# A weight piece loaded as two half transfers, and one head's keys apart from its queries, in an attention kernel

## The chip, the cores and the metric

The kernel runs on one core of one Trainium2 chip. The metric is the device time of one execution in microseconds (us); less is better. The engines are PE (TensorE, matrix multiply), DVE (VectorE), ACT (ScalarE), POOL (GpSimd) and SP (SyncE, which here issues nearly all DMA transfers).

## The reference

Attention over 8 batches, 8 heads, 576 positions and 64 channels, with a bias that is computed from the distance of two positions, and behind it a gated feed-forward layer over all 4608 tokens, whose weights come as 64-bit floats.

```python
scores = scale * np.matmul(q, k.transpose(0, 1, 3, 2)) + bias
attn = np.exp(scores - np.max(scores, axis=-1, keepdims=True))
attn = attn / (np.sum(attn, axis=-1, keepdims=True) + 1e-09)
x = np.matmul(attn, v)          # then heads side by side: (4608, 512)
a = x @ w1
b = x @ w2
h = a * b @ w3
out = (h @ w_out).astype(np.float32)
```

## The kernel before

The kernel has three parts. First the bias of all heads is computed and stored to DRAM (`nb_d`), then comes the attention, and then the feed-forward layer, which keeps PE busy to the end. The change touches the attention only.

**Units.** The attention runs through 32 units: a unit is a pair of heads and one batch. Scores of a unit come in nine tiles, named 0 to 7 and M: an even number belongs to the first head, an odd one to the second, and M holds the last 64 rows of both. For each tile there is a step S (PE: scores from q and k, `op_S`, L332), T (DVE: adds the bias and finds the extreme of each row, L343) and E (ACT: the exponential and its sum, L368). Two tiles at a time are transposed by DVE (R, L378). PE multiplies the transposed tiles with v in the next unit (W0 to W4, L428), ACT copies the product x out of PSUM (X, L437 and L442), and SP stores it (xd, L448).

**Loads.** A unit needs q0 and k0 (first head), q1 and k1 (second head), and v in five parts v0 to v4 (128 or 96 KB), which SP loads with one transfer each (L315), one to two units ahead. POOL copies the lower 64 partitions of a v part to the upper ones (L320). Buffers of q and k stand twice, so a load waits until the scores two units earlier have read them. Most units also load a row of the next pair's bias (L296).

**Weight pieces.** 24 of the 32 units prepare one piece of the weights w_out and w3 (128 x 512 numbers of 64 bits, 512 KB) in nine steps, c0 to c8, made by `narrow`. c0 (`fetch`, L182) is the transfer into `wi`. c1 to c3 run on ACT: the Abs of the high words (`size`, L187), the Copy of the low words (L191), the Sign (L194). c4 to c8 run on POOL (a clamp, three doublings, a sum and a product). Units whose number leaves 0 or 7 when divided by 8 have no piece.

**Order.** The order of all steps is written out by hand. `rhythm` gives each step of a unit a time and an engine, in us from the unit's start (T0), with a unit length of 12.17 us (PERIOD); `arrange` puts the units one behind the other, and every engine, SP's queue too, gets its steps sorted by these times. The times only set the order: an engine that reaches a step waits for what it needs, and all behind it on that engine waits with it. On SP, before: k1 at 9.80, q1 at 9.90 (two units ahead), v2 at 9.85, v3 at 12.10, c0 at 0.2 of the next unit, which is 12.37, v4 at 1.98 of it, xd at 2.80, v0 at 4.55, k0 at 5.50 and q0 at 5.60.

Of the kernel before, what the change touches and what calls it, by code (L numbers as in the profile page):

```python
# [10 lines left out]
I32 = mybir.dt.int32  # L11
# [6 lines left out]
P = 128  # L18
# [13 lines left out]
PERIOD = 12.17  # L32
# [43 lines left out]
def rhythm(tiles, turns):  # L76

    at = {}
    for n, t in enumerate(tiles):
        at["S" + t] = S_AT[n], "PE"  # L80
        at["T" + t] = T_AT[n], "DVE"
        at["E" + t] = E_AT[n], "ACT"
    for n, ts in enumerate(turns):
        at["R" + ts] = R_AT[n], "DVE"
    for n, t in zip("abc", (2.70, 3.36, 4.00)):
        at["r" + n] = PERIOD + t, "DVE"
    at["rd"] = PERIOD + 5.30, "SP"
    for n, w in enumerate(W_AT):
        at[f"W{n}"] = PERIOD + w, "PE"
        at[f"lv{n}"] = w + 1.90 - PERIOD, "SP"  # L90
        at[f"V{n}"] = V_AT[n], "POOL"
    at["X"] = 2 * PERIOD + 0.70, "ACT"
    at["xd"] = 2 * PERIOD + 2.80, "SP"
    for h in range(2):
        for k, n in enumerate("kq"):
            at[f"l{n}{h}"] = -2 * PERIOD + (5.50, 9.80)[h] + 0.1 * k, "SP"
    at["c0"] = 0.2, "SP"
    at["c1"] = 5.60, "ACT"
    at["c2"] = 8.15, "ACT"
    at["c3"] = 11.65, "ACT"  # L100
    at["c4"] = 6.30, "POOL"
    for n, t in zip("567", AT_TWICE):
        at["c" + n] = t, "POOL"
    at["c8"] = 12.80, "POOL"
    return at


def arrange(NU, pieces):

    at = [rhythm(TILES, ("02", "46", "M", "13", "57")) for u in range(NU)]  # L110
    begin(at)
    for n, w in enumerate(W_LAST):
        at[-1][f"W{n}"] = w, "PE"
    at[-1]["X"] = X_LAST, "ACT"
    at[-1]["xd"] = X_LAST + 1.00, "SP"
    for u in range(NU - PER_PAIR):
        b = u % PER_PAIR
        at[u]["n" + TILES[b]] = AT_N, "SP"
        if b == PER_PAIR - 1:
            at[u]["n" + TILES[-1]] = PERIOD + AT_N_LAST, "SP"  # L120
    for k, n in enumerate(("lk0", "lq0")):
        at[2][n] = -2 * PERIOD + 9.60 + 0.1 * k, "SP"
    return {
        (n, u): (u * PERIOD + t + 1.4, e) for u in range(NU) for n, (t, e) in at[u].items() if n[0] != "c" or u in pieces
    }
# [3 lines left out]
def relpos_attention_moe(  # L129
# [17 lines left out]
    nc = tc.nc  # L147
# [3 lines left out]
    NTOK, DO = out.shape  # L151
# [4 lines left out]
    SQ = 8.0  # L156
    assert SQ * SQ == D

    def f(ap):
        return ap.bitcast(F32)  # L160

# [3 lines left out]
    WIDE = moe_w1.dtype == mybir.dt.int64  # L165
    LEAST = struct.unpack("<f", struct.pack("<I", 0x38000000))[0]
    MOST = struct.unpack("<f", struct.pack("<I", 0x47EFFFFF))[0]

    def narrow(pool, src, n, x, queue, pieces=1, clamps=nc.vector, signed=False):

        d = {}

        def cut(ap):
            return ap if pieces == 1 else ap.rearrange("p (c n) -> p c n", c=pieces)

        def fetch():
            if not WIDE:
                queue.dma_start(cut(x), src)
                return
            wi = pool.tile([P, n, 2], I32, name="wi")  # L180
            flat = wi.rearrange("p n t -> p (n t)")
            queue.dma_start(cut(flat), src.bitcast(I32))  # L182
            mag = pool.tile([P, n], F32, name="wmag")
            d.update(lo=wi[:, :, 0], hi=wi[:, :, 1], mag=mag, bits=mag.bitcast(I32))

        def size():
            nc.scalar.activation(d["mag"], f(d["hi"]), AF.Abs)  # L187

        def rest():

            nc.scalar.activation(x, d["lo"].bitcast(U32), AF.Copy, scale=2.0 ** -51, bias=2.0)  # L191

        def sign():
            nc.scalar.activation(f(d["hi"]), f(d["hi"]), AF.Sign)  # L194

        def clamp():
            clamps.tensor_scalar(d["mag"], d["mag"], LEAST, MOST, op0=ALU.max, op1=ALU.min)

        def shift():

            nc.vector.tensor_scalar(d["bits"], d["bits"], 3, None, op0=ALU.logical_shift_left)

        def total():

            nc.gpsimd.tensor_tensor(x.bitcast(I32), x.bitcast(I32), d["bits"], op=ALU.add)
            if not signed:
                nc.gpsimd.tensor_tensor(x, x, f(d["hi"]), op=ALU.mult)

        def mark():

            nc.vector.scalar_tensor_tensor(
                x.bitcast(I32), d["hi"], -2 ** 31, x.bitcast(I32), op0=ALU.bitwise_and, op1=ALU.bitwise_xor,
            )

        def twice():

            nc.gpsimd.tensor_tensor(d["bits"], d["bits"], d["bits"], op=ALU.add)  # L217

        steps = [fetch, size, rest, sign, clamp, shift, total]
        if signed:  # L220
            steps = [fetch, size, rest, clamp, shift, mark, total]
        if clamps is nc.gpsimd:
            steps = steps[:5] + [twice] * 3 + [total]
        return steps if WIDE else [fetch] + [lambda: None] * (len(steps) - 1)

    def drive(plan, *more):
# [15 lines left out]
    w3s = [[held.tile([P, DO], F32, name=f"w3s{t}_{hf}") for hf in range(2)] for t in range(NF)]  # L242
    wos = [held.tile([P, DO], F32, name=f"wos{t}") for t in range(NF)]
    cva = ctx.enter_context(tc.tile_pool(name="cva", bufs=2))
# [14 lines left out]
    vp = []  # L259
    units = [(p, b) for p in range(NPAIR) for b in range(B)]  # L260
    NU = len(units)
    lo, hi = slice(0, 64), slice(64, 128)
    NB = {}
    st = {u: {} for u in range(NU)}

# [84 lines left out]
    for i in range(2):  # L350
        t = att.enter_context(tc.tile_pool(name=f"sums{i}", bufs=1)).tile([P, 64], F32, name=f"sums{i}")
# [98 lines left out]

    def piece_of(i):
        if i < NF:
            return narrow(cva, moe_w_out[i * P:(i + 1) * P, :], DO, wos[i], nc.sync, clamps=nc.gpsimd)
        hf, t = divmod(i - NF, NF)
        return narrow(cva, moe_w3[t * P:(t + 1) * P, hf * DO:(hf + 1) * DO], DO, w3s[t][hf], nc.sync, clamps=nc.gpsimd)

    pieces = dict(zip([u for u in range(NU) if 0 < u % B < B - 1], (piece_of(i) for i in range(3 * NF))))
    assert len(pieces) == 3 * NF

# [20 lines left out]
    with ExitStack() as pro:  # L480
# [29 lines left out]
        def reach(G):  # L510

            return (G + 1) * GR - 1, S - 1 - G * GR
# [9 lines left out]
        for G in range(NGRP):  # L522
            n = max(reach(G)) + 1
# [42 lines left out]
        for G in range(NGRP):  # L566
            at = -LEAD + G * PACE_B
# [38 lines left out]
    def fetch_w(t, m):  # L606

        if m == 0:
            big[t] = bg.tile([P, 4, 2 * P], F32, name="big")
        flat = big[t].rearrange("p s n -> p (s n)")  # L610
        src = (moe_w1, moe_w2)[m].rearrange("(c p) n -> p c n", p=P)[:, :, t * P:(t + 1) * P]
        for step in narrow(cva, src, NC * P, flat[:, m * NC * P:(m + 1) * NC * P], nc.sync, pieces=NC, signed=True):
            step()
            yield
# [242 lines left out]
    for i in range(2 * NF):  # L857
        hf, t = divmod(i, NF)
# [16 lines left out]
    for t in range(NF):  # L875
        t0 = t_f + STEP0 * (t - 3) - LEAD_W * max(0, 3 - t)
        for m, (at0, d) in enumerate((((2.70, 3.35, 3.40, 3.80, 4.10, 4.90), -7.0), ((7.00, 7.65, 7.70, 8.00, 8.40, 9.40), -0.8))):
            size, rest, clamp, shift, mark, total = at0
# [11 lines left out]
    for n in range(NPR * NF):  # L890
# [3 lines left out]
        if p == 0:  # L894
            for j, u in AT_U.items():
                for m in range(2):
                    at(t0 + u + 2.08 * m, plain, cs, j, m)
                for k, d in AT_G.items():
                    if n == 0 and k + j == "gc":
                        d = AT_GC  # L900
# [18 lines left out]
        elif 0 < p < NPR - 1 and ft in (2, 5):  # L919
            i = int(ft > 4)  # L920
# [87 lines left out]
```

## Time and profile before

| | before |
|---|---|
| median of three runs | 1077.39 us (1069.25 to 1078.34) |
| the profiled execution | 1073.51 us |
| its span, first to last instruction | 1071.6 us |
| PE busy (share of the span) | 1038.9 us (97%) |
| DVE | 780.5 us (73%) |
| ACT | 557.4 us (52%) |
| POOL | 318.1 us (30%) |
| moved by DMA | 218.36 MB, mean 204 GB/s |

The shares are averages over the whole span. DVE is busy nine tenths or more of the time through the attention and far less in the feed-forward part, so the attention is to be read by itself. A wait in the views below is idle time of an engine, with what ended it; "issue" stands where nothing that the profile shows ended it. The engines read their instructions by DMA too: q8 is the queue of such transfers, 110 packets of together 1.80 MB in this execution, beside the data queue q1.

### The profile page before, as it was taken

The page shows a single profiled execution, that of the slowest core. Times are in us where ns is not written, and L with a number is a line of the kernel's source. Part 1 is how long each engine was busy: PE and PEld are TensorE (multiplying, and loading weights), DVE is VectorE, ACT ScalarE, POOL GpSimd, SP SyncE. Part 2 cuts the span into 40 slices and gives each one's busy share as a digit, 9 for nine tenths or more (in the row PEclk, how much of TensorE's full clock was granted, in tenths as well). Part 3 has the DMA queues.
Part 4 walks back from the last instruction along what each step waited for, and adds up shares of the span by engine and source line. Part 5 has one row for each costly group of instructions (what it writes and reads, how often), then busy time and mean ns, then how long its engine had stood idle before and what let it go on. Part 6 is the DMA issues. An engine that isn't in the chain of part 4 may idle for free.

```text
span 1071.6 us, 33595 instructions
## 1 busy us (share of the span) xinstructions
PE 1038.9 (97%) x13968; PEld 826.0 (77%) x13968; DVE 780.5 (73%) x1486; ACT 557.4 (52%) x1269; POOL 318.1 (30%) x342
## 2 busy tenths in 40 slices
PE   7979999999999999999899999999999999999998
PEld 2346666666656666688899999999999999999997
DVE  8989999999999999998887455444635545453333
ACT  6958777786777777856553322323323232332222
POOL 0048855873787388664220000000000000000000
PEclk9989999999999999999999999999999999999999
DMA  7977767776776666367857765565575565545431
GB/s 223 293 242 219 213 177 229 212 214 199 211 205 186 184 194 182 116 170 238 272 198 269 252 225 195 198 246 197 181 267 180 196 233 207 197 189 206 143 133 59
DMA packets 93785, 218.36 MB, mean 204 GB/s; under 512 B 22208, under 2 KB 46912, under 8 KB 87488
## 3 DMA queue, kind: packets, MB, share of 16 engines
q1 hardware_dynamic: 93200, 216.19, 62.1%
q8 instruction: 110, 1.80, 0.7%
q14 instruction: 43, 0.35, 0.1%
q10 hardware_dynamic: 432, 0.02, 0.0%
HBM read 171.45 MB, written 44.71 MB: 202 GB/s over the span
## 4 chain that ended last, share of the span: by engine, by line
PE 78%; DVE 10%; issue 5%; DMA 2%; POOL 2%; ACT 2%; SPq 0%; DVEq 0%; POOLq 0%; ACTq 0%
PE X L764 16%; PE acc L428 12%; PE Y L764 12%; PE s L332 11%; PE oc L834 9%; PE od L834 9%; DVE ts L343 4%; PE bacc L552 3%; PE Y L778 3%; DVE pt L378 3%; PE X L778 3%; POOL w3s L673 1%; DMA v<-in_v_dram 1%; DMA nb_d<-bev 1%; ACT pp L368 0%
## 5 line engine op out<-in xcount | busy, mean ns | idle before, releaser
L428 PE MATMUL acc<-pt,v 32*64 32x128 f32 (+1 forms) x9216 | 213.6, 295 | 5.4 <-issue 5.4
L428 PEld LDWEIGHTS acc<-pt,v 32*64 32x64 f32 x9216 | 160.9, 131 | 72.3 <-issue 52.7
L368 ACT ACTIVATE pp<-ts,mx 128x576 f32<-128x576 f32 x256 | 195.9, 766 | 31.5 <-DVE mx L343 30.6
L332 PE MATMUL s<-k,q 64*128 64x288 f32 (+1 forms) x1280 | 195.4, 442 | 9.7 <-DVE mx L343 9.1
L764 PE MATMUL X<-xS,wS 128*128 128x384 f32 x960 | 194.8, 338 | 0.0
L343 DVE CUSTOM_DVE_ANT_0 ts<-s,nb 128x576 f32<-128x576 f32 x256 | 182.9, 738 | 7.3 <-PE s L332 6.9
L378 DVE STREAM_TRANSPOSE pt<-pp 128x1152 f32<-128x1152 f32 x128 | 175.3, 1370 | 4.3 <-ACT pp L368 3.6
L764 PEld LDWEIGHTS X<-xS,wS 128*128 128x128 f32 x960 | 171.5, 188 | 6.8
L332 PEld LDWEIGHTS s<-k,q 64*128 64x128 f32 (+1 forms) x1280 | 90.5, 176 | 79.4 <-issue 35.9
L807 DVE TENSOR_TENSOR wos<-X,wos 128x384 f32<-128x384 f32 x80 | 44.6, 557 | 138.5 <-PE X L764 138.5
L764 PE MATMUL Y<-xS,wS 128*128 128x384 f32 x720 | 145.0, 336 | 0.0
L764 PEld LDWEIGHTS Y<-xS,wS 128*128 128x128 f32 x720 | 127.9, 188 | 0.1
L320 POOL COPY v<-v 64x512 f32<-64x512 f32 (+1 forms) x160 | 87.2, 565 | 119.7 <-DMA v<-in_v_dram 107.0
L811 ACT COPY wos<-X 128x384 f32<-128x384 f32 x80 | 38.4, 480 | 125.9 <-PE X L764 125.9
L787 ACT ACTIVATE ghd<-wos 128x384 fp32r<-128x384 f32 x48 | 25.2, 525 | 124.6 <-DVE wos L807 105.8
L834 PE MATMUL oc<-w3s,ghc 128*128 128x512 f32 x288 | 89.8, 393 | 0.0
L834 PE MATMUL od<-w3s,ghd 128*128 128x512 f32 x288 | 89.6, 392 | 0.0
L807 DVE TENSOR_TENSOR wos<-Y,wos 128x384 f32<-128x384 f32 x80 | 44.6, 557 | 50.2 <-ACT wos L811 36.7
L217 POOL TENSOR_TENSOR wmag<-wmag 128x512 int32<-128x512 int32 x72 | 74.7, 1038 | 5.9
L787 ACT ACTIVATE ghc<-wos 128x384 fp32r<-128x384 f32 x48 | 25.2, 526 | 92.4 <-DVE wos L807 75.7
L834 PEld LDWEIGHTS oc<-w3s,ghc 128*128 128x128 f32 x288 | 53.4, 188 | 8.6
L834 PEld LDWEIGHTS od<-w3s,ghd 128*128 128x128 f32 x288 | 53.5, 188 | 8.5
(95 smaller groups left out, 1399.7 us busy)
## 6 DMA issues: line engine op xcount, KB each, us to landing
wS<-w_d SPq DMA_DIRECT2D x40, 1792.0 KB, 7.6
q<-in_q_dram SPq DMA_DIRECT2D x64, 288.0 KB, 3.7
wi<-in_moe_w_dram SPq DMA_DIRECT2D x32, 512.0 KB, 5.3
w_d<-wS SPq DMA_DIRECT2D x8, 1792.0 KB, 6.3
v<-in_v_dram SPq DMA_DIRECT2D x96, 128.0 KB, 3.4
nb_d<-bev SPq DMA_DIRECT2D x36, 295.5 KB, 3.9
k<-in_k_dram SPq DMA_DIRECT2D x64, 144.0 KB, 3.2
x_d<-x SPq DMA_DIRECT2D x32, 288.0 KB, 4.9
```

The lines of the kernel that those rows point to most:

```text
L217: nc.gpsimd.tensor_tensor(d["bits"], d["bits"], d["bits"], op=ALU.add)
L320: nc.gpsimd.tensor_copy(t[64:128], t[0:64])
L332: nc.tensor.matmul(s[outs, hf, :HS], d[f"q{h}"][rows, q0:q0 + n], d[f"k{h}"][rows, :], start=True, stop=True,)
L343: nc.vector.tensor_tensor_reduce(out=halves(ts), in0=d.pop(("s", t))[:, :, :HS], in1=halves(NB[p, t]), op0=ALU.add, op1=ALU.min, scale=-1. ...
L368: nc.scalar.activation(d["p", ps][:, k * S:(k + 1) * S], ts, AF.Exp, bias=mx, scale=-1.0, accum_out=SUMS[u // 4 % 2][:, col:col + 1],)
L378: nc.vector.transpose(o, st[u].pop(("p", ts)))
L428: nc.tensor.matmul(acc[outs, a, c0:c0 + 32 * (t1 - t0)], d["v", b][rows, h], pt_[rows, t0:t1, 32 * b:32 * b + 32], start=(b == 0), stop=(b ...
L764: nc.tensor.matmul(acc, w[:, l, W_AT[n], i * P:(i + 1) * P], x[:, r, X_AT[n]], start=(k in "125" and i == 0 and m == 0), stop=(i == 1 and ...
L778: nc.tensor.matmul(acc, w[:, l, i * P:(i + 1) * P], x[:, r, 2 * k + "cd".index(j)], start=(n == 0), stop=(n == 11),)
L787: nc.scalar.activation(st[n], st["g" + j], AF.Copy)
L807: nc.vector.tensor_tensor(st[o], x, y, op=op)
L834: nc.tensor.matmul(d["o", j, t], l[:, sl], folded[ft][r], start=(ft == 0 and n == 0), stop=(ft == NF - 1 and n == 2),)
```

## The change

The piece's transfer is cut by partitions. `fetch` (c0) now loads partitions 0 to 63 of the piece, 256 KB, and a new step c9 (`second`) loads partitions 64 to 127. c9 is planned at 2.1 us of the unit, where c0 stays at 0.2 us; both are issued by SP. The Abs (c1) reads both halves. The loads of q and k change their places: of the first head, q goes out just ahead of k where k went out just ahead of q (5.50 and 5.60); of the second head, q goes out at 9.80 us in place of k, and k 2.5 us later, at 12.30 us, just ahead of c0.

```diff
     for h in range(2):
         for k, n in enumerate("kq"):
-            at[f"l{n}{h}"] = -2 * PERIOD + (5.50, 9.80)[h] + 0.1 * k, "SP"
+            at[f"l{n}{h}"] = -2 * PERIOD + (5.50, 9.80)[h] + (0.1, 2.5)[h] * (n == "k"), "SP"
     at["c0"] = 0.2, "SP"
+    at["c9"] = 2.1, "SP"
...
-    def narrow(pool, src, n, x, queue, pieces=1, clamps=nc.vector, signed=False):
+    def narrow(pool, src, n, x, queue, pieces=1, clamps=nc.vector, signed=False, halves_of=False):
...
-            queue.dma_start(cut(flat), src.bitcast(I32))
+            if halves_of:
+                queue.dma_start(flat[lo], src[lo].bitcast(I32))
+            else:
+                queue.dma_start(cut(flat), src.bitcast(I32))
...
+        def second():
+            if halves_of and WIDE:
+                queue.dma_start(d["flat"][hi], src[hi].bitcast(I32))
...
         if clamps is nc.gpsimd:
-            steps = steps[:5] + [twice] * 3 + [total]
+            steps = steps[:5] + [twice] * 3 + [total, second]
```

The steps keep their order on PE, DVE, ACT and POOL; only SP's queue changes. In an even unit with a piece, SP's queue had, from k1 of one unit to the next v0 (wi is the piece, x_d the store of x):

```order
L315 DMA k1_2190<-in_k_dram 128x288
L315 DMA v2_2192<-in_v_dram 64x384
L315 DMA q1_2194<-in_q_dram 128x576
L315 DMA v3_2240<-in_v_dram 64x512
L182 DMA wi_2269<-in_moe_w_out_dram 128x1024
L315 DMA v4_2287<-in_v_dram 64x384
L448 DMA x_d0_88<-x_2277 128x576
L315 DMA v0_2343<-in_v_dram 64x512
```

and has now, at the same place:

```order
L324 DMA q1_2195<-in_q_dram 128x576
L324 DMA v2_2197<-in_v_dram 64x384
L324 DMA v3_2243<-in_v_dram 64x512
L324 DMA k1_2272<-in_k_dram 128x288
L186 DMA wi_2274<-in_moe_w_out_dram 64x1024
L324 DMA v4_2292<-in_v_dram 64x384
L194 DMA wi_2274<-in_moe_w_out_dram 64x1024
L457 DMA x_d0_88<-x_2282 128x576
L324 DMA v0_2349<-in_v_dram 64x512
```

k moved from the front to just ahead of the piece, and the piece's second half stands between v4 and the store of x. At the attention's start, where the bias is just complete, SP's queue had (v of units 0 and 1, nbM the last bias rows, ahead of the first piece):

```order
L315 DMA v0_851<-in_v_dram 64x512
L315 DMA v1_853<-in_v_dram 64x512
L315 DMA v2_858<-in_v_dram 64x384
L279 DMA nbM_827<-nb_d_87 64x576
L280 DMA nbM_827<-nb_d_87 64x576
L315 DMA v3_874<-in_v_dram 64x512
```

and has now:

```order
L324 DMA v0_849<-in_v_dram 64x512
L324 DMA v1_851<-in_v_dram 64x512
L324 DMA k1_856<-in_k_dram 128x288
L288 DMA nbM_825<-nb_d_87 64x576
L289 DMA nbM_825<-nb_d_87 64x576
L324 DMA v2_858<-in_v_dram 64x384
L324 DMA v3_874<-in_v_dram 64x512
```

k1 of unit 1, which went out ahead of the bias before, stands ahead of nbM, and v2 of unit 0 has moved behind nbM.

## Rows read from the trace of the kernel before

**Rows 1.** The page's head: the span

```profile
span 1071.6 us, 33595 instructions
```

**Rows 2.** Windows: length; busy us (instructions) of PE, PEld, DVE, ACT, POOL; clock, DMA, GB/s

```profile
50.00:81.00 31.00, 24.17 (x396) 12.90 (x397) 25.64 (x51) 19.22 (x46) 11.73 (x15) 0.89 0.80 236
81.00:448.00 367.00, 358.67 (x9796) 233.18 (x9793) 360.10 (x707) 282.48 (x696) 257.95 (x290) 1.00 0.68 199
```

**Rows 3.** Waits of DVE, 81 to 448 us: in total, times, longest

```profile
DVE ts L343 <- PE s L332: 4.5, 6, 1.5
DVE pt L378 <- ACT pp L368: 1.2, 3, 0.5
```

**Rows 4.** Waits of PE, 81 to 448 us, then 138.5 to 164.8 (units without piece)

```profile
PE acc L428 <- issue: 5.4, 6, 1.9
PE s L332 <- issue: 0.5, 1, 0.5
...
PE s L332 <- DVE mx L343: 0.2, 1, 0.2
```

**Rows 5.** Timeline of PE: start, us, what, and idle before it in brackets

```profile
123.43 1.24 PE L332 MATMUL s<-k,q 64*128 64x288 f32 x7 [0.55 <-issue]
...
208.17 0.34 PE L428 MATMUL acc<-pt,v 32*64 32x160 f32 x1 [1.12 <-issue]
...
294.57 0.49 PE L428 MATMUL acc<-pt,v 32*64 32x128 f32 x4 [1.14 <-issue]
...
320.94 0.77 PE L428 MATMUL acc<-pt,v 32*64 32x128 f32 x23 [1.88 <-issue]
...
382.12 0.49 PE L428 MATMUL acc<-pt,v 32*64 32x160 f32 x6 [0.75 <-issue]
```

**Rows 6.** Timeline of SP's queue: issues of three of the pieces

```profile
201.11 0.52 SPq L182 DMA_DIRECT2D wi<-in_moe_w_dram  x1
...
313.04 0.54 SPq L182 DMA_DIRECT2D wi<-in_moe_w_dram  x1
...
375.26 0.58 SPq L182 DMA_DIRECT2D wi<-in_moe_w_dram  x1
```

**Rows 7.** DMA, 201.1 to 205.7 us, then 205.7 to 206.7 us: packets and queues

```profile
DMA packets 465, 1.11 MB, mean 241 GB/s; under 512 B 60, under 2 KB 107, under 8 KB 464
q1 hardware_dynamic: 464, 1.10, 80.7%
...
q8 instruction: 1, 0.02, 5.5%
```

**Rows 8.** The page's DMA issues: count, KB each, median us to landing

```profile
q<-in_q_dram SPq DMA_DIRECT2D x64, 288.0 KB, 3.7
wi<-in_moe_w_dram SPq DMA_DIRECT2D x32, 512.0 KB, 5.3
```

**Rows 9.** Waits of ACT, 81 to 448 us; timeline of SP, ACT, DVE, one unit

```profile
ACT wmag L187 <- DMA wi<-in_moe_w_dram: 12.1, 13, 1.5
ACT wmag L187 <- DMA wi<-in_moe_w_out_dram: 3.3, 5, 1.0
...
226.44 0.54 SPq L182 DMA_DIRECT2D wi<-in_moe_w_dram  x1
227.09 0.47 SPq L315 DMA_DIRECT2D v<-in_v_dram  x1
...
232.74 0.69 ACT L187 ACTIVATE wmag<-wi 128x512 f32<-128x512 f32 x1 [1.54 <-DMA wi<-in_moe_w_dram]
...
235.40 0.76 ACT L368 ACTIVATE pp<-ts,mx 128x576 f32<-128x576 f32 x1
...
236.34 1.38 DVE L378 STREAM_TRANSPOSE pt<-pp 128x1152 f32<-128x1152 f32 x1
```

**Rows 10.** Timeline of ACT and DVE at the attention's start

```profile
72.40 0.69 ACT L187 ACTIVATE wmag<-wi 128x512 f32<-128x512 f32 x1 [3.83 <-DMA wi<-in_moe_w_out_dram]
...
74.64 1.38 DVE L378 STREAM_TRANSPOSE pt<-pp 128x1152 f32<-128x1152 f32 x1 [1.96 <-ACT pp L368]
```

More of the change, by code (lines that the diff above doesn't have):

```diff
@@ L157, in relpos_attention_moe @@
     assert SQ * SQ == D
+    lo, hi = slice(0, 64), slice(64, 128)
     def f(ap):
@@ L181, in fetch @@
             flat = wi.rearrange("p n t -> p (n t)")
-            queue.dma_start(cut(flat), src.bitcast(I32))
+            if halves_of:
+                queue.dma_start(flat[lo], src[lo].bitcast(I32))
+            else:
+                queue.dma_start(cut(flat), src.bitcast(I32))
             mag = pool.tile([P, n], F32, name="wmag")
-            d.update(lo=wi[:, :, 0], hi=wi[:, :, 1], mag=mag, bits=mag.bitcast(I32))
+            d.update(flat=flat, lo=wi[:, :, 0], hi=wi[:, :, 1], mag=mag, bits=mag.bitcast(I32))
+        def second():
+            if halves_of and WIDE:
+                queue.dma_start(d["flat"][hi], src[hi].bitcast(I32))
         def size():
@@ L261, in relpos_attention_moe @@
     NU = len(units)
-    lo, hi = slice(0, 64), slice(64, 128)
     NB = {}
@@ L452, in piece_of @@
         if i < NF:
-            return narrow(cva, moe_w_out[i * P:(i + 1) * P, :], DO, wos[i], nc.sync, clamps=nc.gpsimd)
+            return narrow(cva, moe_w_out[i * P:(i + 1) * P, :], DO, wos[i], nc.sync, clamps=nc.gpsimd, halves_of=True)
         hf, t = divmod(i - NF, NF)
-        return narrow(cva, moe_w3[t * P:(t + 1) * P, hf * DO:(hf + 1) * DO], DO, w3s[t][hf], nc.sync, clamps=nc.gpsimd)
+        return narrow(cva, moe_w3[t * P:(t + 1) * P, hf * DO:(hf + 1) * DO], DO, w3s[t][hf], nc.sync, clamps=nc.gpsimd, halves_of=True)
     pieces = dict(zip([u for u in range(NU) if 0 < u % B < B - 1], (piece_of(i) for i in range(3 * NF))))
```

## The prediction

> **What bounds the kernel now.** I read the busy time by stretch first. The change touches the attention alone, which lies between about 50 and 448 us of the span of 1071.6 us [rows 1]. In its even part, 81 to 448 us, PE is busy 358.67 and DVE 360.10 of 367.00 us [rows 2]. Two engines that feed each other are both full, so a stall on either reaches the end; ACT (282.48) and POOL (257.95) have room. Both idle times are short, and that is the most the change can win: next come the waits. DVE waited 4.5 us for scores from PE and 1.2 us for exponentials from ACT, 5.7 us together [rows 3]. PE's own wait in that part is mostly "issue": 5.4 + 0.5 us, in which nothing that the profile shows held it [rows 4]. In a stretch of two units that load no weight piece there is none of it [rows 4]. Five of its seven bubbles, 0.55 + 1.12 + 1.14 + 1.88 + 0.75 = 5.44 us, come behind a weight piece's transfer [rows 5]. Take the end of idle minus its length: 207.05, 319.06 and 381.37 us. The piece was issued at 201.11, 313.04 and 375.26 us [rows 6], so PE ran dry 5.9 to 6.1 us after the issue each time; the other two are alike.
>
> Why it ran dry is in the DMA view. From 201.1 to 205.7 us the data queue q1 moved 464 packets, 1.10 MB, at a mean of 241 GB/s for all queues, and the instruction queue q8 none; in the next microsecond q8 moved one packet [rows 7], and PE went on at 208.17 us [rows 5]. My reading: PE's next block of instructions stood behind the piece and whatever the data queue held. What the program asked for is in the order of q1; when the fetch was asked for, the trace does not show.
>
> **The change, part by part.**
>
> *The fetch.* The piece of 512 KB becomes two of 256 KB with v4 between them. Ahead of the end of the old piece stood k1, v2, q1, v3, piece: 144 + 96 + 288 + 128 + 512 = 1168 KB. Ahead of the end of the first half stand q1, v2, v3, k1, half: 912 KB. That is 256 KB less, and at 241 GB/s [rows 7] 1.1 us less for a fetch that meets it. Each bubble shrinks by up to that: 0.55, 1.12, 1.14 and 0.75 go to about zero, 1.88 to 0.8, so 5.44 becomes 0.8. The second half makes a second heap with v4 before it and x_d behind it (96 + 256 + 288 = 640 KB), planned 1.9 us later, when 1.9 x 241 = 458 KB have drained. That heap is lower than the old one but no longer small, so I add 0.5 us of new bubbles. PE gains 5.44 - 0.8 - 0.5 = 4.1 us, 76%. DVE's 5.7 us [rows 3] come from the same bubbles (its waits for ACT too: ACT's copy of x waits for PE), so 0.76 x 5.7 = **4.3 us gained**. Ends: 0, if fetches don't stand behind q1, and 5.7, if all goes.
>
> The Trainium skill speaks against this term. Its page "DMA: Bandwidth & Descriptors", section "Queues, rings and completion order", says that a DMA engine takes turns between queues packet by packet. By it a fetch waits for a packet of data and not for a heap, and the sum would lack its gain: about 1075 us. The 4.6 us without a q8 packet [rows 7] lean against it, without proving it, since the asking isn't seen; it is the first rival.
>
> *The second half as the last to land.* ACT's Abs (L187) now waits for both halves. Before, the piece landed 5.3 us after its issue (512 KB); q, 288 KB, takes 3.7 us [rows 8], and I take that for a half, no smaller transfer being likely to wait less in this queue. The half is issued behind v4. In the unit shown, the piece went out at 226.44 us and v4 at 227.09 us for 0.47 us [rows 9], so the half would go at 227.6: 1.2 us later, landing 1.2 + 3.7 - 5.3 = -0.4 us, sooner. On the plan's own times it is 1.9 us later, landing +0.3 us. If the queue never runs empty, 96 KB of v4 more stand ahead, and a gap may open between the halves. I take +0.6 us; the ends are -0.4 and +1.9 us (the whole of the plan's delay). What a later Abs costs is read in the unit with the longest wait, 1.54 us [rows 9]: behind Abs stand, in ACT's order, the exponentials of M and 1, the Copy, and the exponential of 3, which ends at 235.40 + 0.76 = 236.16; DVE's transpose of 1 and 3 starts at 236.34. Slack is 0.18 us, and for a wait w it is 1.72 - w. The 18 waits make 12.1 + 3.3 = 15.4 us, 0.86 us on average [rows 9]; I spread them evenly from 0.18 to 1.54, which has that mean. A shift s then costs 18 x (s - 0.18)^2 / (2 x 1.36) = 6.6 x (s - 0.18)^2: at +0.6 **1.2 us lost**, at -0.4 nothing. At +1.9 every unit pays: 18 x (1.9 - 1.72) + 15.4 = 18.6 us.
>
> *The start.* At the first piece ACT waited 3.83 us, and DVE's transpose 1.96 us behind it [rows 10]; nothing covers this. Here the new order puts v2 behind the bias row nbM, and v4 ahead of the second half: 192 KB more before the last byte, 0.8 us at the 236 GB/s of that stretch [rows 2]; 0 if the queue had gaps there. **0.6 us lost.** v2 itself has time, since v3 and v4 stood behind nbM already.
>
> *Edits that cost nothing.* 24 more issues on SP, each about 0.5 us [rows 9]: x_d and the next v0 stand behind the second half, and v0 is planned 2.45 us after it; if SP were late, v0 would be the first to be late, and its copy on POOL is planned 10.6 us after its issue. k1 goes out 2.5 us later; it is first read by the scores of M in the next unit but one, 16.3 us after its issue in place of 18.8 by the plan, against a landing in less than the 3.7 us of q [rows 8]. q before k of one head swaps two neighbours whose first reader is over a unit away. The wait for the last scores that held k1 now holds q1, in the same place. PE, DVE, ACT and POOL keep their order.
>
> **Sum.** The profiled execution took 1073.51 us, its span 1071.6 [rows 1] and 1.9 around it. 1073.5 - 4.3 + 1.2 + 0.6 = 1071.0 us. The three runs had a median of 1077.39 (1069.25 to 1078.34), 3.9 above the profiled one; if those carried more bubbles, more would go, so I do not add the 3.9. **Predicted: 1071.0 us.**
>
> **The rivals.**
> 1. *The fetch does not stand behind the piece; bubbles stay.* For it: the moment of asking isn't seen, and two of seven bubbles have no such piece. Against it: five begin about 6 us after an issue, and none in units without pieces. 1073.5 + 1.2 + 0.6 = 1075.3 us; with fresh luck in the bubbles 1073 to 1079.
> 2. *Slower: ACT's wait for the second half becomes the stall*, in every unit with a piece, at L187, behind it the exponentials and DVE's transposes. It decides from the landing at which it costs 4.3 - 0.6 = 3.7 us, by the formula above 0.93 us later than now; at 1.9 us it costs 18.6: 1073.5 - 4.3 + 18.6 + 0.6 = 1088.4 us. At 1.3 us it costs 8.3, 1078 us. Against it: half the bytes land sooner. The Trainium skill's page "DMA: Bandwidth & Descriptors", section "Rules for kernel authors", advises against two transfers to two partition halves, since both run over the same 16 engines one behind the other. By that, the two halves land no sooner than one, which is this rival at +0.6 to +1.9 us; rows 8 show only that fewer bytes land sooner.
> 3. *More than forecast*: every bubble and every wait of the even part goes, and ACT's slack holds: 1073.5 - 5.7 + 0.6 = 1068.4; if the runs that make the median carried more stalls than the profile, these go too, and the start draws level: 1063 to 1068.
>
> **How the numbers follow.** The forecast has 0.48, rival 1 0.20, rival 2 0.14, rival 3 0.18. The likeliest's own range is 1067 to 1074. To leave out no more than 2 in 10, the range reaches over most of rivals 1 and 3 and the near half of rival 2: 1063.5 to 1079. A measurement of this kernel tells about 1% from no change, here 10.8 us around 1077.39: faster means under 1066.6, slower over 1088.2. Faster is the better part of rival 3: 0.16. Slower is the far end of rival 2: 0.05. The rest, 0.79, is no change that can be told.
>
> **What would show it.** In the profile after: PE's "issue" idle in the even part down from 5.9 to 1 to 2 us, and DVE's waits for PE and ACT from 5.7 to 1 to 2 us; a q8 packet found between the two halves' packets; ACT's waits at the Abs (L187, now L197) up from 15.4 us to 20 to 27; DVE's first long wait at the start near 2.6 us. Units without a piece stay without bubbles. The prediction is wrong if the issue bubbles stay as long (rival 1), or if DVE's idle names ACT's exponentials behind Abs in many units (rival 2).

## The result, and the profile after

The kernel became slower. The median of six runs after is 1089.74 us (1086.28 to 1092.1), that of six runs before beside them 1076.32 us (1069.25 to 1078.34): a ratio of 1.0132, with a 95% interval of 1.0104 to 1.0159. The forecast was 1071.0 us, in a range up to 1079. The profiled execution of after took 1090.33 us. The two medians are 13.4 us apart and the two profiled executions 16.8, since that of before (1073.51 us) lies 2.8 us under its median.

First, where the 16.9 us between the two spans lie. DVE runs the step of tile M (`ts<-s,nbM`) once per unit, so the time from one to the next is the length of a unit:

| from M step to M step | before | after | difference |
|---|---|---|---|
| up to unit 1 | 71.91 | 71.96 | +0.05 |
| unit 1 (the first piece) | 12.21 | 16.98 | +4.77 |
| units 2 to 29 (22 pieces) | 346.35 | 352.65 | +6.30 |
| unit 30 (the last piece) | 11.86 | 16.95 | +5.09 |
| all behind it | 629.30 | 630.01 | +0.71 |

The windows of after, in the columns of [rows 2]; the second window is 10 us longer, because the attention ends later, and it takes in the end of a stall in unit 1 and one in unit 30, both shown further down:

```profile
50.00:81.00 31.00, 21.59 (x292) 11.05 (x298) 23.69 (x47) 17.35 (x43) 9.31 (x13) 0.84 0.83 230
81.00:458.00 377.00, 362.77 (x9704) 233.17 (x9692) 356.28 (x698) 278.51 (x689) 258.11 (x287) 0.99 0.69 192
```

DVE was idle 6.9 us of the even part before, and 20.7 now. The waits of ACT, DVE and PE in it, 81 to 458 us (engine, line, releaser; us in total, times, longest):

```profile
ACT wmag L197 <- DMA wi<-in_moe_w_dram: 27.2, 10, 6.5
ACT wmag L197 <- DMA wi<-in_moe_w_out_dram: 8.3, 5, 2.8
...
ACT wmag L197 <- POOL v L329: 5.7, 5, 1.5
ACT wmag L197 <- issue: 3.8, 1, 3.8
...
DVE ts L352 <- PE s L341: 8.1, 11, 2.9
DVE pt L387 <- ACT ppM L377: 6.9, 4, 3.8
DVE pt L387 <- ACT pp L377: 5.0, 11, 0.7
...
PE acc L437 <- issue: 4.9, 9, 0.9
PE s L341 <- issue: 0.8, 1, 0.8
```

ACT waits 27.2 + 8.3 = 35.5 us at the Abs for a piece, against 15.4 [rows 9]. The six waits that the view puts down to POOL and to "issue" are for the piece too: each ended 0.07 us behind the landing of its second half. So ACT waits 45.0 us there in all, of which 6.55 in unit 30; the counts below are of the first two rows alone, as 35.5 is. DVE's waits for ACT's exponentials (ppM, pp) rose from 1.2 to 11.9 us and those for PE from 4.5 to 8.1 [rows 3]; 3.79 us of the first belong to unit 30 and 2.86 of the second to unit 1. PE's "issue" idle, which the change was to take away, is 5.7 us against 5.9 [rows 4]: the single bubbles are shorter (0.9 against 1.9 us at most), but there are ten and not seven.

The transfers themselves, whole before and in halves after (DMA issues of 81 to 440 us: count, KB, median us to landing):

```profile
wi<-in_moe_w_dram SPq DMA_DIRECT2D x17, 512.0 KB, 5.6
wi<-in_moe_w_out_dram SPq DMA_DIRECT2D x6, 512.0 KB, 5.2
...
wi<-in_moe_w_dram SPq DMA_DIRECT2D x31, 256.0 KB, 4.4
wi<-in_moe_w_out_dram SPq DMA_DIRECT2D x14, 256.0 KB, 4.2
```

In this stretch a half takes 4.4 or 4.2 us where a whole piece took 5.6 or 5.2 (5.3 in [rows 8] is over the whole span): half the bytes save a fifth of the time. From the issues and landings of the pieces in the attention, as means counted from the unit's start (for the second halves without the last piece, which unit 30 shows below): before, the piece was issued at 0.30 and landed at 5.85 us. After, the first half was issued at 0.67 and landed at 4.88, the second was issued at 2.05, took 4.89 and landed at 6.94 us (9.14 at the latest). The last byte that the Abs waits for lands 1.09 us later than before.

**Unit 1.** The timeline of after, and two rows of before behind it (start, us, what; idle before it in brackets):

```profile
67.10 0.70 SPq L186 DMA_DIRECT2D wi<-in_moe_w_out_dram  x1
68.49 0.59 SPq L194 DMA_DIRECT2D wi<-in_moe_w_out_dram  x1
...
75.02 0.67 ACT L197 ACTIVATE wmag<-wi 128x512 f32<-128x512 f32 x1 [6.44 <-DMA wi<-in_moe_w_out_dram]
...
77.23 1.38 DVE L387 STREAM_TRANSPOSE pt<-pp 128x1152 f32<-128x1152 f32 x1 [4.51 <-ACT pp L377]
...
84.33 0.76 DVE L352 CUSTOM_DVE_ANT_0 ts<-s,nb 128x576 f32<-128x576 f32 x1 [2.86 <-PE s L341]
...
79.32 1.33 PE L341 MATMUL s<-k,q 64*128 64x288 f32 x4 [3.68 <-DVE mx L352]
80.59 2.44 PE L437 MATMUL acc<-pt,v 32*64 32x160 f32 x64
...
76.73 0.76 PE L332 MATMUL s<-k,q 64*128 64x288 f32 x4 [1.23 <-DVE mx L343]
79.51 0.76 DVE L343 CUSTOM_DVE_ANT_0 ts<-s,nb 128x576 f32<-128x576 f32 x1 [0.81 <-PE s L332]
```

ACT waits 6.44 us for the first piece where it waited 3.83, and DVE's transpose behind it 4.51 where it waited 1.96 [rows 10]: +2.55 us. PE then stands idle for 3.68 us (1.23 before), and what follows is new: its matmuls run slower (the four of S take 1.33 us, 0.76 before), and DVE waits another 2.86 us for scores, where it waited 0.81. The granted clock shows why (windows of before, then of after, columns as above):

```profile
76.00:79.00 3.00, 2.27 (x70) 1.67 (x72) 2.70 (x8) 2.23 (x6) 2.78 (x4) 1.00 0.76 224
79.00:83.00 4.00, 4.00 (x128) 2.68 (x130) 3.49 (x8) 3.11 (x8) 3.78 (x4) 1.00 0.69 214
...
76.00:79.00 3.00, 0.00 (x0) 0.00 (x0) 1.77 (x2) 2.52 (x7) 2.85 (x3) 0.81 0.74 230
79.00:83.00 4.00, 3.68 (x70) 2.48 (x70) 2.40 (x7) 3.06 (x7) 3.70 (x5) 0.50 0.01 4
83.00:87.00 4.00, 4.00 (x86) 2.54 (x92) 2.67 (x6) 1.36 (x4) 3.62 (x5) 0.79 0.50 139
```

PE ran nothing from 76 to 79 us, and from 79 to 83 it was granted 0.50, the 1.2 GHz level, where before it had 1.00, the 2.4 GHz level.

**Unit 30.** The timeline of SP, ACT, DVE and PE at the last piece:

```profile
436.40 0.47 SPq L186 DMA_DIRECT2D wi<-in_moe_w_dram  x1
441.59 0.39 SPq L188 DMA_DIRECT2D wi<-in_moe_w_dram  x1
442.07 1.57 SPq L324 DMA_DIRECT2D v<-in_v_dram  x1
443.69 0.59 SPq L194 DMA_DIRECT2D wi<-in_moe_w_dram  x1
...
447.97 0.66 ACT L197 ACTIVATE wmag<-wi 128x512 f32<-128x512 f32 x1 [6.55 <-DMA wi<-in_moe_w_dram]
...
449.42 0.78 DVE L387 STREAM_TRANSPOSE pt<-ppM 128x576 f32<-128x576 f32 x1 [3.79 <-ACT ppM L377]
...
450.91 1.33 PE L341 MATMUL s<-k,q 64*128 64x288 f32 x4 [3.18 <-DVE mx L352]
```

Between the halves stands L188, the first weight transfer of the feed-forward part, which takes a buffer that POOL has yet to free:

```profile
SPq L188 <- POOL w3s L217: 4.6, 1, 4.6
```

So the last second half went out 7.3 us behind its first (443.69 - 436.40), and the same fall follows: ACT 6.55, DVE 3.79, PE 3.18 us idle, and from 450 to 457 us the 1.2 GHz level:

```profile
450.00:457.00 7.00, 6.09 (x93) 3.86 (x95) 6.17 (x12) 6.34 (x18) 6.47 (x8) 0.52 0.00 0
```

### The profile page after: what moved, and what is told of

Its sections match the earlier page's. It is cut to its first block, busy times and chain, and to the rows that moved or that the text cites. A ratio compares the mean times of both kernels' runs of the same rounds, so it can differ in the third digit from the quotient of the medians.

```text
span 1088.5 us, 33646 instructions
## 1 busy us (share of the span) xinstructions
PE 1048.4 (96%) x13968; PEld 830.1 (76%) x13968; DVE 781.4 (72%) x1486; ACT 555.9 (51%) x1269; POOL 318.6 (29%) x342
## 4 chain that ended last, share of the span: by engine, by line
PE 74%; DVE 8%; issue 6%; DMA 4%; ACT 3%; POOL 3%; SPq 0%; ACTq 0%; DVEq 0%; POOLq 0%
PE X L773 16%; PE Y L773 12%; PE acc L437 11%; PE s L341 9%; PE oc L843 9%; PE od L843 9%; DVE ts L352 4%; PE bacc L561 3%; PE X L787 3%; PE Y L787 3%; DVE pt L387 3%; DMA wi<-in_moe_w_dram 2%; POOL w3s L682 1%; ACT pp L377 1%; POOL wmag L227 1%
## 5 line engine op out<-in xcount | busy, mean ns | idle before, releaser
L437 PE MATMUL acc<-pt,v 32*64 32x128 f32 (+1 forms) x9216 | 218.1, 297 | 5.7 <-issue 4.9
L437 PEld LDWEIGHTS acc<-pt,v 32*64 32x64 f32 x9216 | 163.2, 132 | 75.9 <-issue 53.2
L341 PE MATMUL s<-k,q 64*128 64x288 f32 (+1 forms) x1280 | 198.5, 447 | 18.0 <-DVE mx L352 16.7
L207 POOL TENSOR_SCALAR wmag<-wmag 128x512 f32<-128x512 f32 x24 | 46.0, 1916 | 62.3 <-ACT wmag L197 47.3
```

The source lines that it names most:

```text
L341: nc.tensor.matmul(s[outs, hf, :HS], d[f"q{h}"][rows, q0:q0 + n], d[f"k{h}"][rows, :], start=True, stop=True,)
L437: nc.tensor.matmul(acc[outs, a, c0:c0 + 32 * (t1 - t0)], d["v", b][rows, h], pt_[rows, t0:t1, 32 * b:32 * b + 32], start=(b == 0), stop=(b ...
```

## The experiments

**Which part costs.** The halves alone, with the old order of the loads, then the order alone with a whole piece:

```diff
-            at[f"l{n}{h}"] = -2 * PERIOD + (5.50, 9.80)[h] + (0.1, 2.5)[h] * (n == "k"), "SP"
+            at[f"l{n}{h}"] = -2 * PERIOD + (5.50, 9.80)[h] + 0.1 * k, "SP"
```

> The piece in two halves as in the change, but k and q go out in the old order. Before takes 1076.3 us, the change 1089.7. Theory A (the second half lands late and ACT's Abs waits for it; the halves alone carry the loss): 1086 to 1091 us, ACT's waits at the Abs of 35 us or more in the even part as in the change (35.5), the last piece's second half still behind a transfer for the next stage. Theory C (the new place of the keys carries it): 1074 to 1079 us.

Measured: 1087.16 us, ratio 1.0086 (1.0055 to 1.0116); ACT waits 32.5 us at Abs in the even part.

> The new order of k and q alone, the piece whole as before. Theory A: no loss, 1073 to 1078 us, ACT's waits at the Abs near the 15.4 us of before. Theory C: most of the 13 us, 1085 us or more. The start has v2 of unit 0 behind the bias row nbM in this kernel too, for up to 1 us.

Measured: 1079.24 us, ratio 1.0018 (0.9987 to 1.005); ACT waits 12.6 us at Abs in the even part. So most of the loss is the halves', and the order alone can't be told from no change. The traces, one of each, show more. With the halves alone unit 1 took 17.13 us, units 2 to 29 took 348.23 and unit 30 took 14.79; with the order alone 16.86, 349.03 and 11.86. Either alone has the stall of unit 1. The +6.30 us of units 2 to 29 in after are +1.88 with the halves alone; whether that is a part of the order's or the luck of one trace, these runs don't show.

**Why: the width of the transfer or its lateness.** A half over 64 neighbouring partitions might be slow in itself. Two kernels cut the piece otherwise and leave the times of issue as in after:

```diff
-                queue.dma_start(flat[lo], src[lo].bitcast(I32))
+                queue.dma_start(flat[:, 0:n], src.bitcast(I32)[:, 0:n])
```

> The change, but each half takes half of the columns of all 128 partitions (2 KB rows) in place of 64 whole partitions. Bytes, places and count of transfers are the same. Theory A1 (a transfer to 64 neighbouring partitions moves its 4 KB rows at about half speed, some 300 ns a row in place of 160, and so lands late): the loss outside the last piece goes, about 4.7 us of it stay there, 1076 to 1081 us, ACT's waits at the Abs near 15 to 22 us. Theory A2 (the second half is late only because it is issued later): 1086 to 1091 us, ACT's waits as in the change.

Measured: 1085.73 us, just under the range of A2, ratio 1.0069 (1.0034 to 1.0104); the second half lands at 6.68 us, ACT waits 31.8 us at Abs.

The other cuts into even and odd partitions:

```diff
-                queue.dma_start(flat[lo], src[lo].bitcast(I32))
+                queue.dma_start(flat[0:P:2], src[0:P:2].bitcast(I32))
-                queue.dma_start(d["flat"][hi], src[hi].bitcast(I32))
+                queue.dma_start(d["flat"][1:P:2], src[1:P:2].bitcast(I32))
```

> The change, but the first half takes the even partitions and the second the odd ones: 64 partitions with 4 KB rows each, spread over all 128. Theory A1 in the form that neighbouring partitions share a way into the memory: as with columns, 1076 to 1081 us. Theory A1 in the form that it is the number of rows or their size in a transfer: as the change, 1086 to 1091 us. Theory A2 (later issue alone): 1086 to 1091 us as well, and then the column halves are slow too.

Measured: 1090.51 us, ratio 1.0103 (1.004 to 1.0166), landing at 6.93 us. However it is cut, the second half lands at 6.7 to 6.9 us and most of the loss stays. Then the time of issue:

```diff
-    at["c9"] = 2.1, "SP"
+    at["c9"] = 0.25, "SP"
```

> The kernel after, the second half put into SP's queue right behind the first (place 0.25 of the unit instead of 2.1). Theory A (the loss is the second half's lateness: it is issued 2.05 us into the unit and lands at 6.94, and in the last piece it stands behind the next stage's first weight transfer): the second half is issued some 0.6 us behind the first, lands near 6.0 to 6.3, ACT's waits at Abs fall from 35.5 to 15 to 20 us, unit 30 comes back from 16.95 to about 12, the whole is 1077 to 1081. Theory B (a piece in two transfers of 64 partitions is itself slower, whenever it is issued): landing stays near 6.9, time 1086 or more.

Measured: 1079.53 us, ratio 1.0008 (0.9975 to 1.0041). The same two transfers of 64 partitions, issued one behind the other, cost nothing that can be told. The second half lands at 6.35 us, unit 30 takes 12.10 us, and ACT's waits at Abs in the even part:

```profile
ACT wmag L197 <- DMA wi<-in_moe_w_dram: 16.0, 16, 2.5
...
ACT wmag L197 <- DMA wi<-in_moe_w_out_dram: 7.1, 7, 2.0
```

23.1 us is more than the 15 to 20 expected, but no wait is over 2.5 us. Units 2 to 29 are at 342.1 us, under before; unit 1 still takes 17.23. Third, the transfers as in after, and the waiting instruction later:

```diff
-    at["c1"] = 5.60, "ACT"
+    at["c1"] = 7.25, "ACT"
-    at["c4"] = 6.30, "POOL"
+    at["c4"] = 7.30, "POOL"
```

> The kernel after, with Abs at 7.25 of the unit instead of 5.60 and the clamp that reads its result at 7.30 instead of 6.30; transfers as in after. Theory A (the loss reaches DVE and PE through ACT's wait at Abs): ACT's waits there fall from 35.5 to under 12 us, DVE's waits in the attention from 20 towards 8, and the time to 1078 to 1083; the last piece keeps its wait of several us, since its second half lands 7 us late. Theory B (the halves cost by other means: PE's fetch bubbles, or other loads made late by them): ACT's waits fall too, but the time stays at 1086 to 1091.

Measured: 1082.61 us, ratio 1.0041 (1.0016 to 1.0066). Waits of ACT at Abs and of DVE, 81 to 458 us:

```profile
ACT wmag L197 <- DMA wi<-in_moe_w_dram: 8.6, 4, 4.8
ACT wmag L197 <- DMA wi<-in_moe_w_out_dram: 1.6, 2, 1.1
...
DVE ts L352 <- PE s L341: 6.7, 10, 2.5
DVE pt L387 <- ACT pp L377: 6.2, 8, 3.9
```

ACT's 35.5 us (45.0 with the six other waits) became 10.2, units 2 to 29 went from 352.65 to 346.97 us, the level of before, and unit 30 kept its 17.00. So the loss of units 2 to 29 goes through ACT's wait at the Abs; the late landing costs only where something waits for it early.

**The two ends.** The first and the last piece whole, the other 22 in halves:

```diff
+        hv = i not in (0, 3 * NF - 1)
...
-            return narrow(cva, moe_w_out[i * P:(i + 1) * P, :], DO, wos[i], nc.sync, clamps=nc.gpsimd, halves_of=True)
+            return narrow(cva, moe_w_out[i * P:(i + 1) * P, :], DO, wos[i], nc.sync, clamps=nc.gpsimd, halves_of=hv)
```

> The kernel after, with the first piece (unit 1) and the last (unit 30) in one whole transfer each; the other 22 in halves. Theory A by units: unit 30 gives back 5.1 us (its second half no longer stands behind the next stage's weight transfer); if the stall of unit 1 comes from the halves, it gives back 4.8 too: 1080. If unit 1 stalls with the whole piece as well, 1084 to 1085. Rival (the loss is spread evenly over the 24 pieces, some 0.55 us each): 1088 to 1089.

Measured: 1084.93 us, ratio 1.0075 (1.0042 to 1.0109). Unit 30 is back at 11.85 us: the last piece's 5.1 us are the halves' alone. Unit 1 still stalls (15.25 us) with a whole first piece and the new order, which is the case for which 1084 to 1085 was expected. Does it stall in the kernel before too? A second trace of that kernel:

> The kernel before, unchanged, traced a second time: its first trace ran 1073.5 us and is some 3 to 4 us under the median of its runs. If the start-up stall (the first piece's ACT wait at Abs 6.4 us instead of 3.8, PE's idle 3.7 us behind it, granted clock 0.5 for 6.8 us from about 78 us) also belongs to ordinary runs of the kernel before, this trace shows it and its time is 1076 to 1079. If the stall comes only with the change, unit 1 is again near 12.2 us and the time near 1073.

Measured: 1075.0 us, unit 1 at 12.43 us, DVE's transpose waiting 2.18 us. No stall. But the kernel before has no firm guard against it, as a later run showed: in e16 (below), whose queue up to there is that of before, the piece landed at 74.2 us against 72.4, and

```profile
76.45 1.38 DVE L378 STREAM_TRANSPOSE pt<-pp 128x1152 f32<-128x1152 f32 x1 [4.04 <-ACT pp L368]
...
82.85 0.76 DVE L343 CUSTOM_DVE_ANT_0 ts<-s,nb 128x576 f32<-128x576 f32 x1 [2.17 <-PE s L332]
```

with unit 1 at 15.81 us. Of four traces with whole pieces, the old order and the first piece in unit 1, one stalls; of the nine with the halves or the new order, all do (14.35 to 17.23 us).

**Does the forecast gain exist?** The start gets in its way, so the first piece is moved from unit 1 to unit 7, which had none: in the kernel before, and in after with the second half at once (the edit of e6).

```diff
-    pieces = dict(zip([u for u in range(NU) if 0 < u % B < B - 1], (piece_of(i) for i in range(3 * NF))))
+    pieces = dict(zip([u for u in range(NU) if u == 7 or (u > 1 and 0 < u % B < B - 1)], (piece_of(i) for i in range(3 * NF))))
```

> The kernel before, its first piece fetched in unit 7 instead of unit 1 (the other 23 as they were). Theory (the first piece's transfer, crossing the start-up loads, costs the kernel before too): ACT's wait of 3.8 us at Abs and DVE's of 1.96 behind it go, unit 1 falls from 12.2 us to about 11.5, unit 7 pays its share of a piece (0 to 0.5): 0 to 1 us faster than before, 1075.5 to 1076.5. Rival (in ordinary runs unit 1 stalls like in the kernel after, and the two traces of before happen to miss it): 4 us faster, near 1072.

Measured: 1074.21 us, ratio 0.9975 (0.9939 to 1.0011), which can't be told from no change; unit 1 at 10.91 us.

> The kernel after with the second half right behind the first and the first piece moved from unit 1 to unit 7. In e6_at_once units 2 to 29 took 342.1 us against 346.4 and 347.4 in the two traces of before, and unit 1 17.2 against 12.2 and 12.4. If these two are all that sets it apart from before (the halves do bring what they were to bring, and the start takes it back), unit 1 falls to about 11.5 and the time is 1079.5 - 5.7 = 1073 to 1075, some 0.2% under before. Rival (the shorter units are one trace's luck): 1077 to 1079.

Measured: 1072.91 us, ratio 0.9954 (0.9925 to 0.9983), the lowest median here of a kernel that leaves all of the computation as it was, 16.8 us under after. Waits of ACT at Abs and of DVE, 81 to 458 us:

```profile
ACT wmag L197 <- DMA wi<-in_moe_w_dram: 14.4, 14, 2.9
ACT wmag L197 <- DMA wi<-in_moe_w_out_dram: 4.5, 6, 1.4
...
DVE ts L352 <- PE s L341: 2.0, 4, 0.7
DVE pt L387 <- ACT pp L377: 1.1, 2, 0.7
DVE pt L387 <- ACT ppM L377: 0.5, 1, 0.5
```

DVE waits 3.6 us, against 5.7 before [rows 3]. Next the Abs at 7.25, in the kernel before and on top of e14:

> The kernel before with Abs at 7.25 of the unit instead of 5.60 and the clamp behind it at 7.30: a whole piece lands at 5.85 on average. If ACT's waits at Abs (15.4 us) carry into DVE's (5.7 us), 2 to 4 us faster, 1072.5 to 1074.5, and PE's fetch bubbles of 5 to 6 us stay. If in the kernel before the stalls come from PE's fetch bubbles alone: no change, 1075.5 to 1077.5, though ACT no longer waits.

Measured: 1075.35 us, ratio 0.9978 (0.9946 to 1.0009). ACT no longer waits at Abs in the even part, and the time can't be told from that of before. In its trace units 2 to 29 took 346.96 us against 346.35, so nearly all of the 15.4 us of waits lay inside the slack.

> All three on the kernel after: second half right behind the first, first piece in unit 7, Abs at 7.25. Theory A (lateness against Abs is what the halves cost): with no wait left at Abs it is at least as fast as e14_at_once_moved, by 0 to 3 us: 1070 to 1074. If Abs moved later costs elsewhere (ACT's exponentials behind it, M's weights copied late): 1075 to 1078.

Measured: 1074.26 us, ratio 0.9976 (0.9946 to 1.0006), no gain over e14, though DVE's idle time in units 2 to 29 fell to 2.3 us (6.9 before, 4.8 in e14). What ate that is a small step that I had not looked at: DVE adds 1e-9 to the sums of the rows in every fourth unit. Its durations in the traces of e6, then e15 (count; ns least/median/most):

```profile
L394 DVE TENSOR_SCALAR sums<-sums x8: 169/178/376, 112.3 to 453.5; 128x36 f32<-128x36 f32 x8
```

```profile
L394 DVE TENSOR_SCALAR sums<-sums x8: 172/1051/1158, 105.6 to 447.8; 128x36 f32<-128x36 f32 x8
...
105.39 1.28 POOL L215 TENSOR_TENSOR wos<-wos,wmag 128x512 int32<-128x512 int32 x1
...
105.55 1.16 DVE L394 TENSOR_SCALAR sums<-sums 128x36 f32<-128x36 f32 x1
```

The step takes 0.18 us alone. In e15 one begins 0.16 us after a POOL operation of the weight piece and ends 0.04 us after that one's end. It came to 3.4 and 4.3 us in units 2 to 29 of the two traces of before, to 2.7 after, 1.5 in e6 and 5.9 in e15, by where POOL's steps happened to fall. Six kernels leave it out:

```diff
-            nc.vector.tensor_scalar(r[:, 0:36], r[:, 0:36], 1e-9, None, op0=ALU.add)
             return
```

> The kernel before without the step that adds 1e-9 to the rows' sums (each sum is at least 1, since the largest exponential of a row is 1, so in 32-bit floats the addition leaves it as it is). Theory C (the step waits for the POOL operation beside it and DVE stands meanwhile): the step's 3.6 to 4.5 us in the attention go, 1076.5 - 4 = 1072 to 1073. Rival (whatever DVE does next waits for POOL in its place): only the step's own 8 x 0.18 = 1.4 us go, 1075.

Measured: 1075.92 us, ratio 0.9993 (0.9963 to 1.0023), a miss for theory C. DVE's busy time in units 2 to 29 fell by 2.8 us (339.5 to 336.7), but this execution stalled in unit 1.

> The kernel after without the same step: 2.8 us of it in the trace of after, so 1089.7 - 2.8 = 1087, 14 us over e16_before_no_add by theory A (lateness of the second half, start, last piece), whatever the step does. If the collision had a part in the loss, the two come closer than 11 us.

Measured: 1088.03 us, ratio 1.0102 (1.0076 to 1.0128), 12.1 us over e16: the loss is there without the step.

> The kernel e14_at_once_moved without the step (3.2 us there): 1072.9 - 3.2 = 1069.7. Against e16_before_no_add at 1072.5, the transfers at once and the moved first piece then bring 2 to 3 us, of which the moved piece 1.3 (unit 1: 10.9 against 12.2 us). If the halves bring nothing at all, it stands 1.3 us under e16; if they bring the forecast 4.3, 5 to 6 us under it.

Measured: 1070.8 us, ratio 0.9946 (0.9921 to 0.9971). That is 5.1 us under e16, the case for which the forecast gain was expected; but e16 has its first piece in unit 1, where its trace stalled, so the comparison with e20 below decides.

> The kernel e15_at_once_moved_abs without the step (6.1 us there, five of eight collide for about 1 us each): 1074.3 - 6.1 = 1068 by theory C. If something else on DVE collides in its place: 1073.

Measured: 1073.06 us, ratio 0.9959 (0.9939 to 0.998). The step went, and PE's bubbles came back: 5.7 us of "issue" from 81 to 436 us against 1.1 in e15. Last, e18 with the whole piece and the old order, and e18 with halves and the old order (the diff of e1):

> The kernel before, first piece in unit 7, the step that adds 1e-9 to the sums left out. If the halves at once and the new order bring the forecast 4.3 us, this runs 4 us over e18_moved_no_add, 1074 to 1076; if they bring nothing, the same as it, 1070 to 1072. DVE's idle time in units 2 to 29 was 6.9, 7.6 and 7.7 us in three traces with whole pieces, and 5.0, 4.8, 2.3, 8.1 and 7.5 us in five with halves at once: a mean 1.9 us apart, so I expect 1072 to 1073.

Measured: 1073.65 us, ratio 0.9951 (0.9926 to 0.9976).

> e18_moved_no_add with k ahead of q as in the kernel before; halves at once. If the order matters little (e2_order alone: 1.0018, from 0.9987 to 1.005, with the stall of unit 1 in its trace), the same as e18 within 2 us: 1069 to 1073. If the order is what keeps the halves cheap, or what costs, it differs by 3 us or more.

Measured: 1070.4 us, ratio 0.9934 (0.9909 to 0.996).

e18 and e20, with halves and with whole pieces, have the same ratio within their intervals (0.9946, 0.9951). The closest pair is e21 and e20, which ran side by side and differ in the halves alone: means of 1070.78 and 1072.45 us, with a 95% interval for the halves from 0.7 us slower to 4.1 us faster. A gain is not shown, and the forecast 4.3 us lies just outside.

## Why the prediction was wrong

**The fetch (-4.3 us): not found.** PE's "issue" idle from 81 to 436 us was 4.5 to 7.1 us in seven traces with whole pieces (mean 5.7), 2.8 to 8.3 in seven with late halves (mean 5.7), and 1.1 to 5.8 in six with halves at once (mean 4.4). Late halves made the longest bubble of a trace shorter (0.7 to 1.7 us in place of 1.4 to 2.3) and the bubbles more (67 in place of 46). That PE waited for its instructions is borne out: each of the 151 bubbles of that stretch in these 20 traces ended 1.0 to 1.7 us after the end of a packet of q8. The step that failed is the heap: I counted bytes ahead of a fetch as if the fetch stood at their end, from five bubbles that began 6 us after an issue. The 4.6 us without a q8 packet [rows 7] hold one of another instruction queue, q14, 0.9 us behind the piece's issue:

```profile
q14 instruction: 1, 0.01, 0.4%
```

And q8 does not stand still behind a piece. In the seven traces with whole pieces 36 of its packets began 2 to 4 us behind a piece's issue and 93 began 4 to 6 us behind it, where an even spread would have some 66 each; in the units without a piece, counted from 0.3 us of the unit, it was 26 and 13. So fetches are held back while a piece comes in, and not stopped. Rival 1 is right that the bubbles stay. The Trainium skill's rule cited there (page "DMA: Bandwidth & Descriptors", section "Queues, rings and completion order"), turns by packet, would leave the idle time as it was; the total, 5.7 us against 5.9, agrees, which does not prove the rule. When a fetch is asked for, no trace here shows, so what sets the length of a bubble stays open.

**The second half (+1.2 us): right mechanism, wrong size.** This is rival 2. I took 3.7 us for a half, from q with 288 KB, and 0.6 us for the shift; measured were 4.89 and 1.09 us. The formula for the slack came near in this trace: 6.6 x (1.09 - 0.18)^2 = 5.5 us, against +6.30 in units 2 to 29. In part that is luck, since in e1, e3, e9 and e4, where the second half landed at 6.7 to 7.0 us, the same units grew by 1.9, 5.1, 9.2 and 10.8 us over 346.35. The shift was mis-sized because I took a transfer's time from its size: with half the bytes I counted on 1.6 us saved, and it was 0.66 (4.89 against 5.55 from issue to landing), while the second half was issued 1.75 us later than the whole piece had been. Why q, with more bytes, still lands in 3.7 us, no run here shows. The Trainium skill's advice against two transfers to partition halves (same page, section "Rules for kernel authors") pointed the right way; e3, cut by columns, and e6, issued at once, show that here it is the second one's lateness and not the partitions that cost.

**The start (+0.6 us): +4.8.** The later landing was sized too small as well (ACT's wait grew by 2.6 us and not by 0.6 to 0.8), but the step that failed is that I let a wait cost its own length. It passed on to PE, PE's idle 3.7 us were followed by the 1.2 GHz level, and DVE's second wait, 2.86 us against 0.81 before, added 2.05. Nor is the start the halves' alone: the new order with a whole piece stalled (e2), and so did the old queue in one trace of four.

**The last piece (0): +5.1 us, missed.** I named x_d and v0 as what stands behind a second half, in the regular unit alone, and did not look at the last one, where the next part's first weight transfer has its place between the halves on SP and waits for a buffer.

**SP's extra issues (0)**: nothing contradicts it. With units 2 to 29, the start and the last piece as measured the sum is 1073.5 + 6.3 + 4.8 + 5.1 = 1089.7 us, the fetch's zero standing in the first term; the profiled execution took 1090.33, and most of the rest lies behind the attention (+0.71). That this is near the far end of rival 2, 1088.4 us, is luck: that sum had a shift of 1.9 us and 18.6 us lost in the regular units, kept the fetch's gain and had nothing for the last piece.

## What to carry to other kernels

Cutting a transfer in two brought its reader nothing here even with the second part issued right behind the first (it landed at 6.35 us, the whole piece at 5.85), and it cost 13 us with the second part issued later: whoever waits for the whole waits for the last issue, and half the bytes took 0.8 to 0.9 of the time. A step that is added in every unit has to be followed through the first and the last unit too, past everything that the queue holds there. Price a stall at its length plus what the clock takes from PE behind it.

## What was not expected of the hardware

- In the trace of after, PE idle for over 3 us in the attention (3.68 us in unit 1, 3.18 in unit 30) was followed by some 7 us at half the granted clock. Unit 1 grew by 4.8 us for 2.55 us of added waiting.
- A DVE operation of 0.18 us on 128x36 numbers took up to 1.28 us beside a POOL operation and ended with it; the other DVE operations of the attention (transposes, reciprocals) kept their durations (1.38 us at most for the large transpose). The Trainium skill, page "SBUF — State Buffer", section "Who interferes with whom", has a rule for this: the two engines share a port pair that one of them holds for a whole instruction. The end 0.04 us after POOL's agrees. Without the step the medians fell by 0.5 to 2.1 us, less than the 2.7 to 5.9 us that it held; the traces of e16 and e19 show other waits (the stall of unit 1, PE's bubbles), and whether these came in its place is not shown.
